# Low-rank mixing as four 32-row tiles in two visits per batch, and loads of q, k, v issued one per slot

## The chip, the cores and the metric

The kernel runs on one core of a Trainium2 chip. The core has TensorE (matmuls, PE in the profile, with its weight loads as PEld), VectorE (DVE), ScalarE (ACT), GpSimd (POOL) and SyncE (SP), which here only issues DMAs. The time is the device time of one execution in microseconds; of the kernel before it is 581.39 us, the median of five runs (579.47 to 582.15). A profiled execution is a run of its own.

## What is computed

The inputs are q, k and v of shape (8 batches, 12 heads, 448 positions, 64), two gains and the weights of a mixer. First comes attention with normalized q and k, then a mixer with a low-rank mixing over positions and a two-layer network over channels:

```python
q_n, k_n = rmsnorm(q, g_q), rmsnorm(k, g_k)
attn = softmax(q_n @ k_n.transpose / sqrt(64))
x = (attn @ v), heads side by side          # (8, 448, 768)
xt = x.transpose(0, 2, 1)
h = xt @ U @ V                              # U (448, 32), V (32, 448): the low-rank mixing
u = x + h.transpose(0, 2, 1)
ch = np.maximum(u @ w_ch1, 0.0) @ w_ch2     # 768 -> 3072 -> 768
out = u + ch
```

The change touches the two lines with h and u, and the loads of q, k and v.

## The kernel before

**Batches woven together.** While the channel network of batch b runs on TensorE ("fill", the generator `mlp`), the attention of batch b+1 and then its mixing are put between the pieces of that fill. The fill comes in chunks of six matmuls; a chunk of the first layer (ph) has 384 columns per matmul in even batches and 512 in odd ones, every other chunk (pa, pb, pe, po: the second layer) has 384. An even batch after the first has 24 + 22 = 46 chunks, 17664 columns in all, an odd one 24 chunks of 512 and 28 of 384, 23040 columns. `weave` places a list of weighted items into this fill: an item's due point is the running sum of weights times the columns allotted, whole chunks are emitted until that point is reached, then the item. The count starts anew for each list. `FA` gives the share of the columns allotted to the attention (its first number for an even fill, its second for an odd one, `FA0` for batch 0), `FM` that allotted to the mixing; the chunks left after that close the batch. The order of instructions on every engine is the order in which this code emits them.

**Attention.** A tile t is four heads, a slot p two heads. A slot consists of scores (L273, two heads as two 64-row tiles of TensorE), exponentials on ScalarE (L278), and the values of the slot before (L299) with a reciprocal and two multiplies on VectorE (L302 to L306). The normalization of later tiles runs beside: squares (L223, ScalarE), sums (L231, VectorE), scale (L244, VectorE, which makes qkn and frees the buffers of q and k). From slot 14 on (`NPE`) the transposes of qkn into qkT are DMA transposes on SP (L261); `gains` (L265, VectorE) then multiplies q's half, and the scores of that slot wait for it. q and k share three load buffers (tag "qk"), v has one (tag "vt").

**SP's queue.** The loads (L198, L209), the DMA transposes of qkT (L261) and of u (L346) and the stores of the output (L380) are all issued by SP in program order; one that waits holds up all behind it. In each odd slot SP gets three loads one after another: q of tile t+2, v of tile t+2, k of tile t+3.

**Mixing.** Each batch's 448 positions are held as four position tiles of 128 rows (`OFFS`; one of them is an edge, of which half the rows belong to the batch). For batches 1 to 7, `mix_t` multiplies each position tile with its part of U into 32 rows of a PSUM tile: position tile i goes to rows 32i to 32i+31, 128 x 32 tiles of TensorE, two halves of 384 channels. ScalarE copies the result to t4b (L325). So the four partial sums over positions lie one below the other, and V4 holds V four times: `mix_u` sums them by the contraction over 128 rows (L337), two matmuls of 384 columns per position tile, into a PSUM tile of the tag "s" (two buffers, shared with the scores). VectorE adds it to x in one operation (L339) and `mix_uT` issues a DMA transpose of that position tile into u (L346). In an even batch the fourth tile, the edge, isn't transposed; an odd batch transposes all four. u is read by the next batch's ph matmuls, all columns at once. Batch 0 has its own way (`mix_a`, `mix_b`), and the four calls of `mix_u` for batch 0 finish its x in the slots 7 to 10.

**Second layer.** `pair` computes two position tiles together with seven products instead of eight: VectorE forms differences and sums of activations between the products (A11 at L429, A12 at L440, act_sum1 and act_sum3 at L399 and L404), adds x to the outputs (o11 at L442, o12 at L455, o21 at L462) and SP stores them in up to three pieces each. PSUM for fill and products has three buffers (tag "mm"); the values use one buffer of the tag "o", except for the last slot's second head.

Of the kernel before, what the change touches and what calls it, by code (L numbers as in the profile page):

```python
# [9 lines left out]
FP32 = mybir.dt.float32  # L10
BF16 = mybir.dt.bfloat16
AX = mybir.AxisListType.X
AF = mybir.ActivationFunctionType
# [4 lines left out]
def kernel(  # L18
# [13 lines left out]
    nc = tc.nc  # L32
    B, H, S, D = q.shape
    dm = H * D
    dh = moe_w_ch1.shape[1]
    rank = moe_U.shape[1]
    assert (B, H, S, D) == (8, 12, 448, 64)

    P = 128
# [3 lines left out]
    KH = dh // P  # L43
    HG = 4
    HALF = dm // 2
    PAD = 64

    OFFS = ([0, 128, 256, 384], [-64, 64, 192, 320])  # L50
# [14 lines left out]
    upool = ctx.enter_context(tc.tile_pool(name="upool", bufs=1))  # L65
    opool = ctx.enter_context(tc.tile_pool(name="opool", bufs=5))
    ps_mm = ctx.enter_context(tc.tile_pool(name="ps_mm", bufs=3, space=bass.MemoryType.PSUM))
    ps_s = ctx.enter_context(tc.tile_pool(name="ps_s", bufs=2, space=bass.MemoryType.PSUM))
    ps_o = ctx.enter_context(tc.tile_pool(name="ps_o", bufs=1, space=bass.MemoryType.PSUM))
# [5 lines left out]
    NC = KH // 2  # L75
    Tw = consts.tile([P, 3, NC, HALF], BF16, name="Tw")
    S1 = consts.tile([P, NC, P], BF16, name="S1")
# [5 lines left out]
    Ub = consts.tile([P, 2, 4, rank], BF16, name="Ub")  # L83
    V4 = consts.tile([P, S], BF16, name="V4")
    Vsh = consts.tile([P, 2, P], BF16, name="Vsh")
# [2 lines left out]
    one = consts.tile([1, 1], FP32, name="one")  # L88
    eps = consts.tile([SP, 1], FP32, name="eps")
    NWARM, NH = 16, 2  # L90
    FA, FM, NPE, FA0 = (0.74, 0.77), 0.09, 14, 0.66
    flat = Tw.rearrange("p f c n -> p (f c n)")
    lent = [0]

    def lend(p, shape, dtype):

        n = 1
        for d in shape:
            n *= d
        n *= 2 if dtype == FP32 else 1  # L100
        a = flat[0:p, lent[0]:lent[0] + n]
        lent[0] += (n + 15) // 16 * 16
        a = a.bitcast(FP32) if dtype == FP32 else a
        names = "abcd"[:len(shape)]
        return a if len(shape) == 1 else a.rearrange(
            f"p ({' '.join(names)}) -> p {' '.join(names)}", **dict(zip(names, shape)))

    EW, VW = [2, PAD + NJ * S + PAD], [HG, NJ, D + 1]
    Es = [consts.tile([SP, *EW], BF16, name=f"E{i}") for i in range(2)] + [lend(SP, EW, BF16)]
# [10 lines left out]
    def setup():  # L120
# [5 lines left out]
        for t in Es:  # L126
            nc.gpsimd.memset(t[:, :, 0:PAD], 0.0)
            nc.gpsimd.memset(t[:, :, PAD + NJ * S:], 0.0)
        for t in xss:
# [14 lines left out]
    Uc = lend(SP, [NJ * rank], BF16)  # L144
    UT = lend(rank, [PAD + S + PAD], BF16)
    Vf = lend(P, [S], FP32)
# [12 lines left out]
    def setup_u(step):  # L159
        if step == 0:  # L160
            pt = ps_mm.tile([rank, S], BF16, tag="mm")
            for j in range(NJ):
                nc.tensor.transpose(pt[:, j * SP:(j + 1) * SP], Uc[:, j * rank:(j + 1) * rank], ident[:SP, :SP])
            nc.vector.tensor_copy(UT[:, PAD:PAD + S], pt)
        else:
            pt = ps_mm.tile([P, 2, 4, rank], BF16, tag="mm")
            for par in range(2):
                for i, off in enumerate(OFFS[par]):
                    nc.tensor.transpose(pt[:, par, i, :], UT[:, PAD + off:PAD + off + P], ident[:rank, :rank])
            nc.vector.tensor_copy(Ub, pt)  # L170
# [8 lines left out]
    def load_w2(half, i):  # L179
        c, d = slice(8 * i, 8 * (i + 1)), slice(half * HALF, (half + 1) * HALF)  # L180
        nc.gpsimd.dma_start(w2b[:, c, d], w2r[:, c, d])


    NT, NP = B * 3, B * 6
# [125 lines left out]
    t4s, us = {}, {}  # L310

    def x_tiles(b):
        xs = xss[(b // 2) % 2]
        full = [x3_of[b][:, i, :] for i in range(3)]
        return full + [xs] if b % 2 == 0 else [xs] + full

    def mix_t(b):
        xt = x_tiles(b)
        t4b = upool.tile([P, dm], BF16, tag="t4b", name="t4b")
        pm = ps_s.tile([P, 2, 512], FP32, tag="s", name="pm")  # L320
        for half in range(2):
            for i in range(4):
                nc.tensor.matmul(pm[i * rank:(i + 1) * rank, half, 0:HALF], Ub[:, b % 2, i, :],
                                 xt[i][:, half * HALF:(half + 1) * HALF], start=True, stop=True)
        nc.scalar.activation(t4b.rearrange("p (h n) -> p h n", h=2), pm[:, :, 0:HALF], AF.Copy)  # L325
        t4s[b] = t4b

    def mix_u(b, i, halves=(0, 1)):

        par, off = b % 2, OFFS[b % 2][i]  # L330
        lhsT = V4[:, off:off + P] if 0 <= off < 384 else Vsh[:, par, :]
        rows = slice(0, P) if 0 <= off < 384 else slice(64 * par, 64 * par + 64)
        xt = x_tiles(b)[i]
        n, hs = len(halves), slice(halves[0] * HALF, (halves[-1] + 1) * HALF)
        pu = ps_s.tile([P, 2, 512], FP32, tag="s", name="pu") if b else ps_mm.tile([P, n, HALF], FP32, tag="mm")
        for k, half in enumerate(halves):
            nc.tensor.matmul(pu[:, k, 0:HALF], lhsT, t4s[b][:, half * HALF:(half + 1) * HALF], start=True, stop=True)  # L337
        xv = xt[rows, hs].rearrange("p (h n) -> p h n", h=n)
        nc.vector.tensor_add(xv, pu[rows, 0:n, 0:HALF], xv)  # L339

    def mix_uT(b, i):
        par, off = b % 2, OFFS[b % 2][i]
        if i == 0:
            us[b] = upool.tile([P, KD, 384 + 128 * par], BF16, tag="u", name="u")
        if par or off < 384:
            nc.sync.dma_start_transpose(us[b][:, :, i * P:(i + 1) * P],  # L346
                                        x_tiles(b)[i].rearrange("t (c d) -> t c d", d=P))
# [168 lines left out]
    def attention(b, extra={}):  # L516

        items = []

        def add(weight, fn, *args):  # L520
            items.append((weight, lambda: fn(*args)))

        def idle():
            pass

        def sums(p, n):
            f = {12: 0, 13: 1, 14: 3, 15: 2}.get(p)
            if f is not None:
                add(0, weight_sums, f, 3 * n)

        for p in range(b * 6, b * 6 + 6):
            t, odd = divmod(p, 2)
            more, more2 = t + 1 < NT, t + 2 < NT
            add(2 if p == 6 else 1, scores, p, (0, 1))
            add(0, expo, p, 0)
            add(.5, expo, p, 1)
            if p + 1 < NP and (p + 1 >= NPE or not odd):
                add(.5, transposes, p + 1)
            if 7 <= p <= 10:
                add(0, mix_u, 0, p - 7, (0,))  # L540
            sums(p, 0)
            if not odd and more:
                add(0, squares, t + 1, ALL, (1,))
            if odd and more2:
                add(0, squares, t + 2, ALL, (0,))
            if p % 6:
                add(2, values, p - 1, 0)
            elif b > 1:
                add(1, idle)
            sums(p, 1)  # L550
            if not odd and more:
                add(0, reduce, t + 1, ALL, (1,))
            if odd and more:
                add(0, scale, t + 1, 1)
                add(0, yield_port, t + 1, 1)
                add(0, cast_v, t + 1)
            if odd and p > 6:
                if 6 <= t + 2 < NT:
                    add(0, load, t + 2, 1, (1,))
                    add(0, load_v, t + 2)  # L560
                if t + 3 < NT:
                    add(0, load, t + 3, 1, (0,))
            add(1, scores, p, (2, 3))
            add(0, expo, p, 2)
            add(.5, expo, p, 3)
            if p + 1 < NPE and odd:
                add(.5, transposes, p + 1)
            if 7 <= p <= 10:
                add(0, mix_u, 0, p - 7, (1,))
            if p + 1 < NP:  # L570
                add(0, gains, p + 1)
            if not odd and more:
                add(0, rsqrt, t + 1)
            sums(p, 2)
            if p % 6:
                add(1.5, values, p - 1, 1)
            elif b > 1:
                add(1, idle)
            sums(p, 3)
            if not odd and more:  # L580
                add(0, scale, t + 1, 0)
                add(0, yield_port, t + 1, 0)
            if odd and more2:
                add(0, reduce, t + 2, ALL, (0,))
            if p in extra:
                add(0, *extra[p])
        add(2, values, b * 6 + 5, 0)
        add(2, values, b * 6 + 5, 1)
        return items
# [145 lines left out]
            nc.scalar.activation(hT[:, 2 * i:2 * i + 2, 0:384], ph[:, :, 0:384], AF.Relu)  # L735

    def mixing(b):
        items = [(1, lambda: mix_t(b))]
        for i in range(4):
            items.append((1, lambda i=i: (mix_u(b, i), mix_uT(b, i))))  # L740
        return items

    def weave(fill, total, items):
# [62 lines left out]
```

## Time and profile before

| | |
|---|---|
| median of five runs | 581.39 us (579.47 to 582.15) |
| the profiled execution | 583.15 us, its span 581.4 us, mean granted clock 0.991 |
| TensorE busy | 563.1 us, 97% of the span |
| VectorE, ScalarE, GpSimd busy | 397.0, 280.6, 78.4 us |
| ph matmuls (L488) | 1107, 231.0 us |
| mixing: pu matmuls (L337) | 64, of 326 ns each; those of 384 columns for batches 1 to 7 are 56 of them |
| mixing: additions on VectorE (L339) | 28 of 768 columns, 0.95 us each, and 8 of 384, 0.55 us each |
| mixing: copy to t4b (L325) | 7 of 0.81 us |
| DMA transposes | 34 of qkT, 3.2 us median from issue to landing; 25 of u, 2.8 us |
| loads of q, k, v on SP | 448 KB each, 3.9 to 6.2 us median from issue to landing |

Busy time of TensorE counts a matmul from its start to its modelled end, and matmuls overlap in the pipeline; where TensorE follows at full rate, the distance of the starts is the cost. "Idle before" in a timeline's brackets is time in which the engine had nothing in flight, with what ended it. A wait in SP's own queue is no loss in itself, as SP mostly has nothing to do.

### The profile page before, as it was taken

How to read it: one execution, taken by the hardware profiler on the slowest of the kernel's cores; microseconds unless marked ns; L12 is line 12 of the kernel's file. 1: busy time of each engine (PE TensorE's matmuls, PEld its weight loads, DVE VectorE, ACT ScalarE, POOL GpSimd, SP SyncE). 2: the span in 40 equal slices, each digit the busy share in tenths (PEclk: the TensorE clock that was granted, in tenths of full speed). 3: DMA queues.
4: the chain of work that ended last, by engine and by line, in shares of the span. 5: the costliest groups of instructions: out<-in, count | busy, mean ns of one | idle time of the engine just before them, and what ended most of it. 6: DMA issues, size and time to landing. Idle time of an engine off the chain costs nothing.

```text
span 581.4 us, 11339 instructions
## 1 busy us (share of the span) xinstructions
PE 563.1 (97%) x4590; PEld 307.8 (53%) x4613; DVE 397.0 (68%) x811; ACT 280.6 (48%) x413; POOL 78.4 (13%) x122
## 2 busy tenths in 40 slices
PE   7899999999999999999999999999999999999997
PEld 2465556544465555544456555544456555554464
DVE  5867987389975687747777498756767587453342
ACT  5865673177621876166651677237661386302200
POOL 5651421000020001000020001000002010000010
PEclk9789999999999999999999999999999999999999
DMA  8999998515563355635536355556245431040021
GB/s 215 248 240 235 207 172 161 126 39 104 112 167 83 82 122 112 156 85 119 120 79 137 86 125 117 145 118 121 60 92 158 104 96 33 29 109 0 1 55 54
DMA packets 103648, 67.22 MB, mean 116 GB/s; under 512 B 54716, under 2 KB 102060, under 8 KB 103596
## 3 DMA queue, kind: packets, MB, share of 16 engines
q1 hardware_dynamic: 93988, 56.77, 41.8%
q0 software_dynamic: 9376, 9.44, 10.0%
q8 instruction: 36, 0.59, 0.4%
q10 hardware_dynamic: 232, 0.30, 0.2%
q14 instruction: 16, 0.13, 0.1%
HBM read 52.19 MB, written 11.01 MB: 109 GB/s over the span
## 4 chain that ended last, share of the span: by engine, by line
PE 84%; DVE 7%; DMA 4%; ACT 3%; issue 1%; POOL 1%; DVEq 0%; POOLq 0%; ACTq 0%
PE ph L488 34%; PE pb L413 10%; PE o L299 7%; PE pe L413 7%; PE po L413 7%; PE sc L273 7%; PE pa L413 6%; DMA qkT<-qkn 3%; ACT E L278 2%; PE pu L337 2%; DVE qkn L244 2%; PE warm L759 1%; PE pt L257 1%; PE first L732 1%; DMA u<-x 1%
## 5 line engine op out<-in xcount | busy, mean ns | idle before, releaser
L488 PE MATMUL ph<-u,w1b 128*128 128x384 bf16 (+1 forms) x1107 | 231.0, 353 | 1.5
L278 ACT ACTIVATE E<-sc 112x896 bf16<-112x896 f32 x184 | 160.1, 915 | 59.9 <-PE sc L273 58.3
L488 PEld LDWEIGHTS <-w1b 128*128 128x128 bf16 x1128 | 102.8, 98 | 108.6 <-issue 22.5
L413 PEld LDWEIGHTS <-hT 128*128 128x128 bf16 x1080 | 101.3, 98 | 71.5 <-issue 8.8
L491 ACT ACTIVATE hT<-ph 128x384 bf16<-128x384 f32 (+1 forms) x95 | 51.5, 543 | 136.2 <-PE ph L488 134.4
L493 DVE TENSOR_SCALAR hT<-ph 128x512 bf16<-128x512 f32 (+1 forms) x93 | 57.9, 622 | 53.2 <-PE ph L488 52.5
L299 PEld LDWEIGHTS <-E 112*128 112x128 bf16 x1472 | 59.8, 99 | 16.9 <-issue 1.9
L299 PE MATMUL o<-va,E 112*128 112x65 bf16 x1440 | 62.3, 196 | 0.8 <-DVE xs L306 0.8
L273 PE MATMUL sc<-qkT 64*128 64x448 bf16 x384 | 56.8, 362 | 4.8 <-ACT E L278 1.6
L244 DVE TENSOR_TENSOR qkn<-qk,rstd 112x512 bf16<-112x512 f32 x84 | 55.7, 701 | 8.0 <-ACT rstd L237 4.2
L720 POOL COPY scratch<-qkn 1x1 bf16<-1x1 bf16 x44 | 11.7, 265 | 311.0 <-DVE qkn L244 302.5
L413 PE MATMUL po<-w2b,hT 128*128 128x384 bf16 x288 | 52.5, 326 | 0.6 <-DVE hT L493 0.6
L231 DVE TENSOR_REDUCE rstd<-sq 112x16 f32<-112x1024 f32 x40 | 48.5, 1212 | 4.8 <-ACT sq L223 4.1
L413 PE MATMUL pa<-w2b,hT 128*128 128x384 bf16 x264 | 49.5, 326 | 0.0
L413 PE MATMUL pb<-Tw,hT 128*128 128x384 bf16 x264 | 48.0, 326 | 0.0
L223 ACT ACTIVATE sq<-qk 112x1024 f32<-112x1024 f32 x36 | 38.3, 1063 | 2.3 <-issue 1.1
L303 DVE TENSOR_TENSOR x<-o,rec 128x192 bf16<-128x192 f32 x96 | 34.3, 357 | 3.7
L448 POOL TENSOR_TENSOR o<-o,x 128x384 f32<-128x384 f32 x11 | 12.6, 1144 | 161.2 <-DVE o L447 161.2
L302 DVE RECIPROCAL rec<-o 128x4 f32<-128x4 f32 x96 | 17.0, 177 | 24.6 <-PE o L299 24.2
L273 PEld LDWEIGHTS <-qkT 64*128 64x128 bf16 x384 | 12.7, 94 | 36.8 <-issue 31.8
L428 ACT ACTIVATE pb<-pa 128x384 f32<-128x384 f32 x11 | 5.2, 475 | 50.4 <-PE pa L413 50.4
L339 DVE TENSOR_TENSOR x<-pu,x 128x768 bf16<-128x768 f32 (+1 forms) x27 | 23.3, 865 | 7.2 <-PE pu L337 7.0
(106 smaller groups left out, 450.7 us busy)
## 6 DMA issues: line engine op xcount, KB each, us to landing
qk<-in_k_dram SPq DMA_DIRECT2D x21, 448.0 KB, 6.2
vt<-in_v_dram SPq DMA_DIRECT2D x20, 448.0 KB, 5.1
qk<-in_q_dram SPq DMA_DIRECT2D x19, 448.0 KB, 3.9
w2b<-in_moe_w_ch_dram POOLq DMA_DIRECT2D x6, 768.0 KB, 9.4
w1b<-in_moe_w_ch_dram POOLq DMA_DIRECT2D x2, 1536.0 KB, 21.1
out_dram<-o SPq DMA_DIRECT2D x15, 168.0 KB, 2.7
out_dram<-o SPq DMA_DIRECT2D x16, 144.0 KB, 2.1
out_dram<-o SPq DMA_DIRECT2D x15, 120.0 KB, 2.5
```

Of the source, the lines that this page charges most:

```text
L223: nc.scalar.activation(sqs[t, s][:, hs], qks[t, s][:, hs], AF.Square)
L231: nc.vector.tensor_reduce(rstds[t][:, s, hs].rearrange("p h j -> p (h j)"), sqs[t, s][:, hs].rearrange("p h (j d) -> p (h j) d", d=D), AX, ...
L244: nc.vector.tensor_tensor(qkn[:, s].rearrange("p j h d -> p h j d"), qks[t, s][:, hp].rearrange("p h (j d) -> p h j d", d=D), rstd[:, s, h ...
L273: nc.tensor.matmul(sc[:, hh, 0:S], kT[pp, kc * SP:kc * SP + P], qT[pp, :], start=True, stop=True)
L278: nc.scalar.activation(E_of(p)[:, :, PAD + kc * S:PAD + (kc + 1) * S], scs.pop((p, kc))[0:SP, :, 0:S], AF.Exp, scale=float(D) ** 0.5)
L299: nc.tensor.matmul(o[:, i, :], E[:, hh, c:c + P], va[:, hl, kc, :], start=(kc == 0), stop=(kc == NJ - 1))
L303: nc.vector.tensor_tensor(x3[:, :, d0:d0 + D], o[:, t0:t0 + 3, 0:D], rec[:, t0:t0 + 3].rearrange("p c -> p c ()").to_broadcast([P, 3, D]), ...
L339: nc.vector.tensor_add(xv, pu[rows, 0:n, 0:HALF], xv)
L413: nc.tensor.matmul(ps, lhs[:, c, :], rhs[:, c, :], start=first and c == 0, stop=last and c == NC - 1, skip_group_check=again)
L488: nc.tensor.matmul(ph, w1b[:, dc, hc * P:(hc + 1) * P], u[:, dc, :], start=(dc == 0), stop=(dc == KD - 1))
L491: nc.scalar.activation(hT[:, hc, 0:n], ph, AF.Relu)
L493: nc.vector.tensor_relu(hT[:, hc, 0:n], ph)
```

## The change

Three things are changed together.

- `mix_t` sums over the position tiles in PSUM instead of laying them below each other. Now rows 32j to 32j+31 hold channel block j (192 channels), and the four position tiles accumulate there: 16 matmuls of 192 columns instead of 8 of 384. The result t4b has 192 columns instead of 768. It lies in the buffer of the tag "o".
- `mix_us` takes two position tiles per visit. For each it runs four matmuls with 32 rows of contraction, one per channel block j, on the four row tiles of TensorE, each into a PSUM bank of its own (two PSUM tiles of the tag "s" with two banks each). VectorE then adds them to x in two operations of 384 columns per position tile, and the DMA transposes follow per position tile. The items' weights are 0.4, 1.2 and 2.0 instead of five ones, FA falls by 0.02 and FM rises by 0.02.
- The loads of a tile go out one at a time: k of tile t+2 in the even slot, behind that slot's transposes; q of tile t+2 in the odd slot where the three were; v of tile t+2 at the end of the odd slot.

```diff
--- before.py
+++ after.py
@@ -43,6 +43,7 @@
     KH = dh // P
     HG = 4
     HALF = dm // 2
+    BLK = dm // 4
     PAD = 64
 
 
@@ -88,7 +89,7 @@
     one = consts.tile([1, 1], FP32, name="one")
     eps = consts.tile([SP, 1], FP32, name="eps")
     NWARM, NH = 16, 2
-    FA, FM, NPE, FA0 = (0.74, 0.77), 0.09, 14, 0.66
+    FA, FM, NPE, FA0 = (0.72, 0.75), 0.11, 14, 0.66
     flat = Tw.rearrange("p f c n -> p (f c n)")
     lent = [0]
 
@@ -316,14 +317,33 @@
 
     def mix_t(b):
         xt = x_tiles(b)
-        t4b = upool.tile([P, dm], BF16, tag="t4b", name="t4b")
-        pm = ps_s.tile([P, 2, 512], FP32, tag="s", name="pm")
-        for half in range(2):
-            for i in range(4):
-                nc.tensor.matmul(pm[i * rank:(i + 1) * rank, half, 0:HALF], Ub[:, b % 2, i, :],
-                                 xt[i][:, half * HALF:(half + 1) * HALF], start=True, stop=True)
-        nc.scalar.activation(t4b.rearrange("p (h n) -> p h n", h=2), pm[:, :, 0:HALF], AF.Copy)
+        t4b = upool.tile([P, BLK], BF16, tag="t4b", name="t4b", padded_shape=[P, dm])
+        pm = ps_o.tile([P, BLK], FP32, tag="o", name="pm", padded_shape=[P, 4 * (D + 1)])
+        for i in range(4):
+            for j in range(4):
+                nc.tensor.matmul(pm[j * rank:(j + 1) * rank, :], Ub[:, b % 2, i, :],
+                                 xt[i][:, j * BLK:(j + 1) * BLK], start=(i == 0), stop=(i == 3))
+        nc.scalar.activation(t4b, pm, AF.Copy)
         t4s[b] = t4b
+
+    def mix_us(b, i0):
+
+        par = b % 2
+        pus = [ps_s.tile([P, 2, 512], FP32, tag="s", name="pu") for _ in range(2)]
+        for k in range(2):
+            off = OFFS[par][i0 + k]
+            edge = not 0 <= off < 384
+            for j in range(4):
+                r = slice(j * rank, (j + 1) * rank)
+                nc.tensor.matmul(pus[j // 2][:, j % 2, k * BLK:(k + 1) * BLK],
+                                 Vsh[r, par, :] if edge else V4[r, off:off + P], t4s[b][r, :], start=True, stop=True)
+        for k in range(2):
+            off = OFFS[par][i0 + k]
+            rows = slice(0, P) if 0 <= off < 384 else slice(64 * par, 64 * par + 64)
+            for h in range(2):
+                xv = x_tiles(b)[i0 + k][rows, h * HALF:(h + 1) * HALF].rearrange("p (j n) -> p j n", j=2)
+                nc.vector.tensor_add(xv, pus[h][rows, :, k * BLK:(k + 1) * BLK], xv)
+            mix_uT(b, i0 + k)
 
     def mix_u(b, i, halves=(0, 1)):
 
@@ -539,6 +559,8 @@
             if 7 <= p <= 10:
                 add(0, mix_u, 0, p - 7, (0,))
             sums(p, 0)
+            if not odd and p > 7 and t + 2 < NT:
+                add(0, load, t + 2, 1, (0,))
             if not odd and more:
                 add(0, squares, t + 1, ALL, (1,))
             if odd and more2:
@@ -554,12 +576,8 @@
                 add(0, scale, t + 1, 1)
                 add(0, yield_port, t + 1, 1)
                 add(0, cast_v, t + 1)
-            if odd and p > 6:
-                if 6 <= t + 2 < NT:
-                    add(0, load, t + 2, 1, (1,))
-                    add(0, load_v, t + 2)
-                if t + 3 < NT:
-                    add(0, load, t + 3, 1, (0,))
+            if odd and p > 6 and 6 <= t + 2 < NT:
+                add(0, load, t + 2, 1, (1,))
             add(1, scores, p, (2, 3))
             add(0, expo, p, 2)
             add(.5, expo, p, 3)
@@ -582,6 +600,8 @@
                 add(0, yield_port, t + 1, 0)
             if odd and more2:
                 add(0, reduce, t + 2, ALL, (0,))
+            if odd and p > 6 and 6 <= t + 2 < NT:
+                add(0, load_v, t + 2)
             if p in extra:
                 add(0, *extra[p])
         add(2, values, b * 6 + 5, 0)
@@ -735,9 +755,9 @@
             nc.scalar.activation(hT[:, 2 * i:2 * i + 2, 0:384], ph[:, :, 0:384], AF.Relu)
 
     def mixing(b):
-        items = [(1, lambda: mix_t(b))]
-        for i in range(4):
-            items.append((1, lambda i=i: (mix_u(b, i), mix_uT(b, i))))
+        items = [(.4, lambda: mix_t(b))]
+        for i in (0, 2):
+            items.append((1.2 + .4 * i, lambda i=i: mix_us(b, i)))
         return items
 
     def weave(fill, total, items):
```

## Prediction

> **What bounds the kernel now.** I read the page first (busy shares, the chain that ended last), then the busy time by stretch, then the timeline of one mixing and of the slots before it.
>
> ```profile
> span 581.4 us, 11339 instructions
> ...
> PE 563.1 (97%) x4590; PEld 307.8 (53%) x4613; DVE 397.0 (68%) x811; ACT 280.6 (48%) x413; POOL 78.4 (13%) x122
> ...
> PE 84%; DVE 7%; DMA 4%; ACT 3%; issue 1%; POOL 1%; DVEq 0%; POOLq 0%; ACTq 0%
> ```
>
> TensorE is busy 97% of the span and 84% of the chain. So only two things can move the time: columns that TensorE no longer streams, and gaps between its matmuls. The stretches tell where the gaps are.
>
> ```profile
> 188.00:250.00 62.00, 60.03 (x529) 34.05 (x528) 45.62 (x93) 34.33 (x51) 5.57 (x10) 1.00 0.55 119
> 290.00:325.00 35.00, 35.00 (x287) 20.50 (x286) 24.29 (x49) 9.68 (x16) 4.40 (x5) 1.00 0.47 109
> 325.00:385.00 60.00, 59.13 (x523) 33.78 (x523) 45.53 (x93) 33.85 (x51) 5.57 (x10) 1.00 0.54 123
> ```
>
> The columns are length, then PE, PEld, DVE, ACT and POOL busy. The two stretches in which batches 2 and 4 fill TensorE leave 1.97 and 0.87 us idle, the one from an odd batch's fill 0.00. The granted clock is 1.00 in all three. Now the cause in the first one, from its timeline:
>
> ```profile
> 214.88 0.31 SPq L198 DMA_DIRECT2D qk<-in_q_dram  x1
> ...
> 216.73 0.31 SPq L209 DMA_DIRECT2D vt<-in_v_dram  x1
> ...
> 217.15 0.43 SPq L198 DMA_DIRECT2D qk<-in_k_dram  x1
> ...
> 217.67 1.22 SPq L261 DMA_TRANSPOSE qkT<-qkn  x1
> ...
> 224.80 0.34 DVE L265 TENSOR_SCALAR qkT<-qkT,gg 128x448 bf16<-128x448 bf16 x1 [1.36 <-DMA qkT<-qkn]
> ...
> 225.28 0.55 PE L273 MATMUL sc<-qkT 64*128 64x448 bf16 x4 [0.63 <-DVE qkT L265]
> ```
>
> Three loads of 448 KB go out on SP within 3 us, and the transpose queued behind them lands late. VectorE stands in front of the gain multiply (1.36 us), TensorE behind it (0.63). The chain gives the transposes' flight: 7.11 us here, 2.97 us for one with no load in front.
>
> ```profile
> 217.67 7.11 DMA qkT<-qkn
> ...
> 229.70 2.97 DMA qkT<-qkn
> ```
>
> And the mixing itself, with the boundary to the next batch:
>
> ```profile
> 238.33 0.34 PE L323 MATMUL pm<-x,Ub 128*32 128x384 bf16 x3
> ...
> 238.51 0.33 PE L323 MATMUL pm<-x,Ub 128*32 128x384 bf16 x3
> ...
> 238.77 1.15 PE L413 MATMUL pb<-Tw,hT 128*128 128x384 bf16 x6
> ...
> 239.76 0.49 PE L337 MATMUL pu<-t4b,Vsh 128*128 128x384 bf16 x2
> ...
> 240.08 1.14 PE L413 MATMUL pb<-Tw,hT 128*128 128x384 bf16 x6
> ...
> 243.66 0.49 PE L337 MATMUL pu<-t4b,V 128*128 128x384 bf16 x2
> ...
> 243.86 0.96 DVE L440 TENSOR_TENSOR hT<-hT 128x1536 bf16<-128x1536 bf16 x1
> ...
> 244.73 0.55 DVE L442 TENSOR_TENSOR o<-pa,x 128x384 f32<-128x384 f32 x1
> ...
> 245.20 0.95 DVE L339 TENSOR_TENSOR x<-pu,x 128x768 bf16<-128x768 f32 x1
> ...
> 246.64 1.21 SPq L346 DMA_TRANSPOSE u<-x  x1
> ...
> 249.83 1.46 PE L488 MATMUL ph<-u,w1b 128*128 128x512 bf16 x5
> ```
>
> To be seen: a position's two matmuls (pu) cost TensorE 0.32 us (239.76 to 240.08). The last position is computed at 243.66, its transpose goes out at 246.64, and the next batch's first matmul, which needs all of u, starts at 249.83.
>
> **The change part by part.**
>
> (1) *Mixing on TensorE.* Full rate is 1.95 us for 12 matmuls of 384 columns (chain, "pe L413 x12"), 162 ns each, so 81 ns for 192 columns. The four pm matmuls of a half start within 0.01 us and the next four 0.17 us later: column tiles run together. After them the old code has 8 pu matmuls per batch, 4 x 0.325 = 1.30 us, full width, without a change of tiling. A change of tiling costs: the six pe matmuls from 237.26 should end at 238.24, pm starts 0.09 later; pm takes 0.44 to the next product where two waves need 0.325; together 0.2 us a block. New: per visit two waves of four matmuls with 32 rows, 2 x 81 ns + 0.2 + some 0.03 of issue = 0.39 us, against 0.65 for two old positions. This supposes that four row tiles run together; the scores (two 64-row tiles) do, as their block of four takes 0.49 us (251.22 to 251.71) where four serial passes would need 0.76. Saved 0.26 x 14 visits (batches 1 to 7) = 3.6 us. The projection (mix_t) becomes four waves of 81 ns in place of two of 162; its weight loads (94 ns each) could hold a wave a little, so I add 0.05 x 7. Term: -3.3 us. Bounds: -4.1 (no issue cost, no weight hold) and +3.1 (row tiles run one by one: 8 x 81 ns + 0.2 = 0.85 a visit). I take the value near the scores, the nearest row.
>
> The Trainium skill, "TensorEngine Tiling (Array Packing)", section Tiling Modes, says that changing the tiling mode drains TensorE (key properties), which speaks against this change, as each visit now switches there and back. The trace agrees with 0.2 us around pm. The page's theoretical speedup (section Overview) of up to 4 for 32 rows would make the 1.30 us into 0.33 and the term -6.8; the drains measured in this trace cut it to about half.
>
> (2) *Loads between the transposes.* The k load for tile t+3 leaves the group of three and is issued after the next slot's transpose; v stays behind q, as in most slots SP has nothing else between. The next transpose thus queues behind two loads instead of three; a third of 7.11 - 2.97 = 4.1 us is 1.4, and by the landings in the median (k 6.2 us, v 5.1, issued 0.4 apart) 1.5. The multiplies that now wait 1.1 to 1.9 us (the view of waits: 6.6 us in 5 waits of DVE on qkT) come through nearly on time. No buffer wait is added: k's buffer was freed a slot before, so SP is blocked for less. What is late next: ScalarE's squares of k, now about one slot (some 7 us at 217) after the load's issue instead of two; the load needs 4 to 6. At a batch's first slot the load goes out at about 190.0 (transpose at 188.76 plus 1.27), the squares come at 196.16: enough for 4, just not for 6.2, and then ScalarE (55% busy there) absorbs most. Of the 2.84 us idle in the two stretches, 0.24 at 202.04 and its twin in batch 4 are VectorE's own backlog and stay: 2.84 - 0.48. Term: -2.3 us, bounds 0 and -2.8. The waits at 233.94 (0.52) and 235.77 (0.17) count in it: there the transpose stands behind an output store and now moves ahead of it by a chunk.
>
> (3) *Two positions per visit at the batch boundary.* Even fill, counted in chunks of 384 columns: 46 in all. Old: attention takes 0.74 x 17664 columns, 35 chunks; the last position follows chunk 40. New: 34 chunks, mixing due after 216, 864 and 1943 columns more, chunks 35, 37 and 40. So the last visit stays where it was, six chunks (5.85 us) before the next batch, but it holds two positions with four additions. From s = 243.66: A12 s+0.2, o11 s+1.07, additions of 128x384 (0.55 us, one each 0.47) at s+1.54, 2.01, 2.48, 2.95. SP issues o11's two stores from s+1.9 to 2.9, then the transpose of position 2 (1.21 us; formerly before the stores) at 3.0 and that of position 3 at 4.3; landing 2.8 us after (median of the DMA issues) is s+7.1. TensorE is there at s+6.2. So 0.85 us of stall at each of three boundaries (into batches 3, 5, 7): +2.5 us. Bounds 0 (DMA quicker) and +5 (flight 3.6). Odd fill: visit after chunk 44 of 52 instead of 45, eight left, and the even batch's u needs only position 2: nothing. Batch 0's fill: likewise, nothing.
>
> (4) *The projection's inputs.* Attention ends a chunk or two earlier. In even fills the last values now fall just behind VectorE's A11 (0.96 us); their four small operations (0.6 us) end some 0.2 us after TensorE could start mix_t. In odd fills o12 and act_sum3 (0.55 + 0.94) come before them: about 0.1. Term: +0.7 with rounding (3 x 0.2 + 3 x 0.05), bounds 0 and +2.
>
> (5) *Others.* t4b's eviction shrinks on ScalarE from 0.81 us to below the 0.48 of a copy of 384 columns: hidden, as the additions follow two chunks later. VectorE does 8 additions of 0.55 for 4 of 0.95 per batch, +0.6 us; behind TensorE except in (3). pm in the o buffer: its last reader feeds the same x, no new wait. Denser attention: +0.1, bounds 0 and +1.5.
>
> Sum: -3.3 - 2.3 + 2.5 + 0.7 + 0.1 = -2.3 us. The profiled execution took 583.15 us, 1.77 around its span, and stands 1.8 above the median 581.39. So 580.85 for it, **579.1** as a median. 0.3% (1.7 us) is about what the runs here can tell from no change: five of them spread over 2.7 us.
>
> **The rivals.**
>
> A. *u late eats the gain.* At the last boundary of the trace the chain has 3.44 us of flight for u's last transpose (from 515.51), and TensorE already waits some 0.3 us at 518.99. With that flight everywhere, 1.5 us a boundary instead of 0.85, +2.0: 581.1, no change. For it: stores share the queue there. Against it: at 246.64 the flight fits into the 3.19 us up to 249.83.
>
> B. *The loads change nothing.* VectorE's waits are replaced by others (a backlog as at 202.04, ScalarE waiting for k): the 2.3 are lost, 581.4. For it: VectorE is 74% busy in that stretch. Against it: in the stretches of odd batches, where the transposes are in time, TensorE doesn't wait.
>
> C. *Slower: four row tiles do not run together.* Only two 64-row tiles are seen to. Serial, term 1 is +3.1 instead of -3.3: 585.5. It decides from a visit of about 0.67 us on (579.1 + 14 x 0.28 = 583.0); with pairs in step, 0.52 a visit, the time is 580.9.
>
> D. *All good.* Boundaries in time, everything else as above: 576.6.
>
> **How the numbers follow.** Forecast and D: 0.52 (0.40 and 0.12), all faster. A and B with C's half case: 0.25, the same. C in full, or A at flight times over 4 us at all boundaries together with the upper end of (4) (about 584): 0.23, slower. The range leaves out the most extreme of D and part of C: 575.5 to 584.5; the forecast's own is 577.5 to 580.7.
>
> **What would show it.** Right: pu matmuls of 32x128 starting within 0.02 us four by four and a visit of 0.35 to 0.45 us; transposes of qkT in no case over 5.5 us in flight; the wait at 225 gone; before the first ph of batches 3, 5, 7 a wait for DMA u of 0.5 to 1.2 us. Wrong: pu starts 80 ns apart (C); ScalarE waiting for qk loads; DVE waiting for qkT as before (B); boundary waits above 1.5 us (A) or none (D). What would make the forecast wrong most easily is that terms 1 and 3 nearly cancel and both rest on timings not in the trace.

## The result and the profile after

The changed kernel takes 582.93 us (median of 44 runs, 580.19 to 589.03), the kernel before 581.37 us (79 runs): a ratio of 1.0027, with a 95% interval of 1.0019 to 1.0036. It is 1.6 us slower, 1.1 to 2.1. The forecast was 2.3 us faster. The time lies in the forecast's range, but it moved the other way.

The profiled executions seem to say the opposite: the span is 580.1 us after and 581.4 before. The stretch of the head, which the change doesn't touch, explains it. Busy time by stretch, the kernel before:

```profile
13.00:49.00 36.00, 31.37 (x366) 18.57 (x367) 27.59 (x72) 23.19 (x31) 19.22 (x20) 0.86 1.14 241
```

and the kernel after (the third number from the end is the granted clock):

```profile
13.00:49.00 36.00, 30.78 (x382) 18.31 (x385) 29.51 (x76) 24.85 (x36) 19.10 (x21) 1.00 1.14 240
```

In the execution before, TensorE had 0.86 of its clock in this stretch, and its first chunk of the first layer (ph) starts at 48.86 us instead of 46.62. From there to the last matmul it is 528.7 us before and 529.7 after: 1.0 us slower, the same way as the timed runs. All that follows compares parts from such a landmark to the next, or ratios of timed runs.

The busy shares of the page, the changed kernel:

```profile
span 580.1 us, 11590 instructions
...
PE 557.9 (96%) x4702; PEld 303.5 (52%) x4725; DVE 394.5 (68%) x839; ACT 276.6 (48%) x413; POOL 75.3 (13%) x122
...
PE 82%; DVE 11%; ACT 3%; DMA 2%; issue 2%; POOL 1%; DVEq 0%; POOLq 0%; ACTq 0%
```

TensorE is busy 5.2 us less than before, 0.6 of it in the head, but is not done sooner: VectorE's share of the chain went from 7 to 11%. Busy time by stretch shows where TensorE stands now (length, then PE busy):

```profile
188.00:250.00 62.00, 60.26 (x545) 33.70 (x546) 45.52 (x98) 33.52 (x52) 4.97 (x10) 1.00 0.56 125
290.00:325.00 35.00, 34.84 (x292) 19.87 (x291) 22.22 (x47) 10.34 (x16) 3.80 (x5) 1.00 0.48 109
325.00:385.00 60.00, 58.12 (x532) 32.76 (x532) 44.26 (x97) 31.39 (x49) 4.97 (x10) 1.00 0.49 121
```

Idle are 1.74, 0.16 and 1.88 us (before 1.97, 0.00 and 0.87). The gaps have new places. The timeline of the mixing in the fill of batch 2:

```profile
232.41 0.36 DVE L304 TENSOR_TENSOR x<-o,rec 128x192 bf16<-128x192 f32 x1
...
232.59 0.26 PE L324 MATMUL pm<-xs,Ub 128*32 128x192 bf16 x3
...
232.78 0.23 DVE L307 TENSOR_TENSOR xs<-o,rec 64x64 bf16<-64x64 f32 x1
...
233.06 0.24 PE L324 MATMUL pm<-xs,Ub 128*32 128x192 bf16 x1 [0.21 <-DVE xs L307]
...
233.48 1.15 PE L433 MATMUL pe<-Tw,S 128*128 128x384 bf16 x6
...
238.84 0.34 PE L338 MATMUL pu<-t4b,V 32*128 32x192 bf16 x8
238.95 0.96 DVE L460 TENSOR_TENSOR hT<-hT 128x1536 bf16<-128x1536 bf16 x1 [0.47 <-PE pa L433]
...
239.83 0.55 DVE L462 TENSOR_TENSOR o<-pa,x 128x384 f32<-128x384 f32 x1
240.29 1.94 DVE L345 TENSOR_TENSOR x<-pu,x 128x384 bf16<-128x384 f32 x4
240.40 1.59 SPq L400 DMA_DIRECT2D out_dram<-o  x2
...
242.09 2.54 SPq L366 DMA_TRANSPOSE u<-x  x2
...
246.28 1.46 PE L508 MATMUL ph<-u,w1b 128*128 128x512 bf16 x5 [1.14 <-DMA u<-x]
```

Three things are to be seen. The projection starts at 232.59, gets three matmuls out, and stands until VectorE has written the last x (232.78 + 0.23), so that its fourth starts at 233.06. The second visit's eight matmuls at 238.84 are short: the next product starts 0.28 us later. And behind that visit stand, in this order, A12, o11, the four additions, o11's two stores and two transposes; TensorE is through its work at 244.98 (the last twelve matmuls start at 243.03 and take 1.95) and starts the next batch at 246.28. In the list of waits this is a new line (by the starts, the kernel before loses 0.3 us at the last boundary and nothing at the others):

```profile
PE ph L508 <- DMA u<-x: 4.1, 3, 1.7
```

VectorE's wait for qkT behind a DMA (6.6 us before) has gone from that list. The chain gives the flight of the transpose that ends each of the three boundaries, 2.8 us twice and 4.2 at the last:

```profile
243.39 2.76 DMA u<-x
...
378.83 2.79 DMA u<-x
513.53 4.18 DMA u<-x
```

### The profile page after: what moved, and what is told of

Its sections match the earlier page's. It is cut to its first block, busy times and chain, and to the rows that moved or that the text cites. A ratio compares the mean times of both kernels' runs of the same rounds, so it can differ in the third digit from the quotient of the medians.

```text
span 580.1 us, 11590 instructions
## 1 busy us (share of the span) xinstructions
PE 557.9 (96%) x4702; PEld 303.5 (52%) x4725; DVE 394.5 (68%) x839; ACT 276.6 (48%) x413; POOL 75.3 (13%) x122
## 4 chain that ended last, share of the span: by engine, by line
PE 82%; DVE 11%; ACT 3%; DMA 2%; issue 2%; POOL 1%; DVEq 0%; POOLq 0%; ACTq 0%
PE ph L508 34%; PE po L433 8%; PE pb L433 8%; PE pa L433 8%; PE sc L274 7%; PE o L300 7%; PE pe L433 6%; DVE qkn L245 2%; ACT E L279 2%; DMA u<-x 2%; DVE rstd L232 1%; DVE x L304 1%; DVE hT L424 1%; PE warm L779 1%; DVE hT L460 1%
## 5 line engine op out<-in xcount | busy, mean ns | idle before, releaser
L300 PEld LDWEIGHTS <-E 112*128 112x128 bf16 x1472 | 58.4, 98 | 15.5 <-DVE xs L307 1.3
L245 DVE TENSOR_TENSOR qkn<-qk,rstd 112x512 bf16<-112x512 f32 x84 | 57.7, 724 | 6.8 <-issue 3.3
L300 PE MATMUL o<-va,E 112*128 112x65 bf16 x1440 | 61.0, 194 | 0.0
L740 POOL COPY scratch<-qkn 1x1 bf16<-1x1 bf16 x44 | 8.9, 202 | 307.5 <-DVE qkn L245 303.9
L433 PE MATMUL pa<-w2b,hT 128*128 128x384 bf16 x264 | 47.1, 327 | 0.0
L433 PE MATMUL pe<-Tw,S 128*128 128x384 bf16 x132 | 24.3, 327 | 0.0
L433 PE MATMUL pb<-w2b,hT 128*128 128x384 bf16 x132 | 23.8, 327 | 0.0
```

Source lines behind the costliest of these rows:

```text
L245: nc.vector.tensor_tensor(qkn[:, s].rearrange("p j h d -> p h j d"), qks[t, s][:, hp].rearrange("p h (j d) -> p h j d", d=D), rstd[:, s, h ...
L300: nc.tensor.matmul(o[:, i, :], E[:, hh, c:c + P], va[:, hl, kc, :], start=(kc == 0), stop=(kc == NJ - 1))
L433: nc.tensor.matmul(ps, lhs[:, c, :], rhs[:, c, :], start=first and c == 0, stop=last and c == NC - 1, skip_group_check=again)
```

## The experiments

Read from the two traces by the distances of TensorE's starts, the change is a sum of four terms: tiles -3.5 us, gaps around qkT and the values -2.1, waits for u +4.3, waits in the projection +2.2. These are first readings; the runs below put the tiles at -3.8 and the projection at +2.5. The experiments undo or repair one of them each. Ratios are to the kernel before, timed beside it; 0.1% is 0.58 us.

### The loads alone

```diff
-            if odd and p > 6:
-                if 6 <= t + 2 < NT:
-                    add(0, load, t + 2, 1, (1,))
-                    add(0, load_v, t + 2)
-                if t + 3 < NT:
-                    add(0, load, t + 3, 1, (0,))
+            if not odd and p > 7 and t + 2 < NT:
+                add(0, load, t + 2, 1, (0,))
...
+            if odd and p > 6 and 6 <= t + 2 < NT:
+                add(0, load, t + 2, 1, (1,))
...
+            if odd and p > 6 and 6 <= t + 2 < NT:
+                add(0, load_v, t + 2)
```

> The kernel before with nothing but the moved loads (k in the even slot, q and v in the odd one); mixing, FA and FM are the old ones. Theory T (the change is a sum of four terms, read from the two profiles: tiles -3.5 us, loads -2.1, waits for u at three boundaries +4.3, waits in the projection's matmuls +2.2): 2.1 us faster than before, 579.3, and VectorE's waits for qkT (6.6 us in the kernel before) under 2 us. Rival L (the loads give nothing; the gaps of batch 2 in the profile before belong to that one execution or come back elsewhere): 581.4, no change.

Measured: 0.9992 (0.9974 to 1.0009), 0.5 us faster and not told from nothing. The waits of VectorE in this run:

```profile
DVE qkT L265 <- DMA qkT<-qkn: 3.9, 3, 1.8
```

Of 6.6 us in five waits 3.9 us in three are left, where under 2 was expected. The gap before the scores at 225 us is gone, those in front of the values in the fills of batches 2 and 4 (0.39 and 0.34 us at 232 and 234, 0.42 and 0.34 at 367 and 369) stayed. So the rival is nearer: with the old attention the loads are worth little, and those other gaps are not theirs.

### The mixing with the old loads

```diff
-            if not odd and p > 7 and t + 2 < NT:
-                add(0, load, t + 2, 1, (0,))
...
+            if odd and p > 6:
+                if 6 <= t + 2 < NT:
+                    add(0, load, t + 2, 1, (1,))
+                    add(0, load_v, t + 2)
+                if t + 3 < NT:
+                    add(0, load, t + 3, 1, (0,))
```

> The changed kernel with the loads put back where they were, three together in the odd slot. Theory T: the loads' 2.1 us are lost, 585.0 against 582.9 of the changed kernel, 0.6% slower than before. Rival L: 582.9, as the changed kernel.

Measured: 1.0113 (1.0089 to 1.0138), 6.6 us slower than before and 5.0 slower than the changed kernel. Both theories missed: the loads are worth 0.5 us in the old kernel and 5.0 in the new one. The timeline shows what they prevent there:

```profile
212.20 0.31 SPq L199 DMA_DIRECT2D qk<-in_q_dram  x1
...
214.05 0.31 SPq L210 DMA_DIRECT2D vt<-in_v_dram  x1
...
214.47 0.43 SPq L199 DMA_DIRECT2D qk<-in_k_dram  x1
...
214.99 11.52 SPq L262 DMA_TRANSPOSE qkT<-qkn  x2
...
222.84 0.34 DVE L266 TENSOR_SCALAR qkT<-qkT,gg 128x448 bf16<-128x448 bf16 x1 [2.60 <-DMA qkT<-qkn]
...
223.32 0.55 PE L274 MATMUL sc<-qkT 64*128 64x448 bf16 x4 [2.33 <-DVE rec L303]
```

The flights in its chain:

```profile
214.99 7.83 DMA qkT<-qkn
...
353.41 8.02 DMA qkT<-qkn
```

It is the picture of the kernel before, with TensorE standing 2.33 us instead of 0.63; at 361.94 it is 1.89 again. Not all of the 5.0 us is waiting: in this trace the granted clock falls just after the first of these gaps, to 0.67 from 224 to 226 us and 0.50 from 226 to 228, which lost some 1.7 us by an estimate from these two rows. No such drop follows the gap at 361.94. In all six timed runs of this kernel the mean clock lies between 0.994 and 0.997, while 18 of the 29 runs of the kernel before beside it have 0.999 or more, so such a drop probably belongs to most of them; what sets it off was not tested. The scores come earlier, the transpose doesn't. New in this kernel are the mixing and the denser attention (FA); the next two runs tell which.

### The denser attention alone, and with the loads

```diff
-    FA, FM, NPE, FA0 = (0.74, 0.77), 0.09, 14, 0.66
+    FA, FM, NPE, FA0 = (0.72, 0.75), 0.11, 14, 0.66
```

In the kernel before, first with its old loads:

> The kernel before with FA 0.72 and 0.75 and FM 0.11, and nothing else: old mixing, old loads. Tells what the denser attention does by itself with three loads in front of a transpose. Theory D (the waits for qkT at 223 and 362 us in the run with the mixing only, 2.5 and 2.1 us, come from the denser attention): the same two waits here, and the gaps before the values in batches 2 and 4 (0.65 + 0.34 and 0.41 + 0.34 us) gone: +4.5 - 0.9 - 1.7 = +1.9, 583. Rival: the waits belong to the new mixing; 579.5 to 581, no wait for qkT above 1 us.

Measured: 1.0015 (0.9989 to 1.0041). The time is not told from either, the list of waits is:

```profile
DVE qkT L265 <- DMA qkT<-qkn: 4.8, 5, 1.4
...
PEld L273 <- DMA qkT<-qkn: 3.8, 3, 1.6
```

TensorE now waits for the transposes itself (3.8 us; before 1.6), in the old mixing too: 1.28 us at 225, 1.40 at 361, some 0.57 each at 345 and 353. The gaps in front of the values are gone, as expected. From the first ph to the last matmul this trace takes 530.6 us, 1.9 more than before, but one execution each doesn't settle it. Then with the moved loads:

> The kernel before with the moved loads and the new FA and FM, and the old mixing: everything of the change but the mixing. Theory D (the denser attention is what the loads' move pays for): the waits for qkT of the run with FA alone (1.28, 1.40, 0.56 and 0.58 us lost at TensorE) are gone and the gaps before the values stay gone, 3.8 us faster than that run, ratio to the kernel before about 0.995, 578.5. What is then left of the change, the mixing in two visits, costs -3.5 + 4.3 - 0.5 + 2.2 = +2.5 us on top. Rival: the loads are worth 0.6 us here as in the run with the loads only, ratio 1.000.

Measured: 0.9977 (0.9955 to 0.9999), 1.3 us faster than before, about half of what was expected; in its list of waits there is none for a transpose of qkT. From one batch's first chunk to the next, its trace takes 60.58 us for each of the fills of batches 2 and 4 (before 62.73 and 61.50). From the first ph to the last matmul it takes 526.4 us, 2.3 less than before; the trace of before may hold more of these gaps than its usual run, which no run here settles. In this trace the moved loads and the denser attention belong together: the denser attention removes the gaps in front of the values, the moved loads keep qkT in time for it. Everything but the mixing is a gain of 1.3 us (0.1 to 2.6), and the mixing costs the difference to 1.0027: 2.9 us, where -3.5 + 4.3 - 0.5 + 2.2 = 2.5 was expected.

### The last visit one chunk earlier

```diff
-    FA, FM, NPE, FA0 = (0.72, 0.75), 0.11, 14, 0.66
+    FA, FM, NPE, FA0 = (0.72, 0.75), 0.108, 14, 0.66
```

> The changed kernel with FM 0.108 instead of 0.11. By the due points this moves one thing: in the three even fills the second visit comes after chunk 39 instead of 40, so ahead of A12, of o11 and of o11's stores; every other item stays. Theory T: the wait for u before the first ph of batches 3, 5 and 7 (1.14 us idle in the first, 4.3 us of lost starts in all) is gone, and a wait of up to 0.3 us per even batch for the score buffers at the second visit may come: 4.3 - 0.6 = 3.7 us faster than the changed kernel, 579.2. Rival Q (the flight of the transposes and SP's queue set the boundary, not the order behind A12 and the stores): the wait for u stays above 0.7 us each, 581 or more.

Measured: 0.9968 (0.9947 to 0.9988), 3.4 us faster than the changed kernel. Its timeline in the same place:

```profile
237.88 0.53 PE L338 MATMUL pu<-t4b,V 32*128 32x192 bf16 x8
...
238.30 4.57 SPq L366 DMA_TRANSPOSE u<-x  x3
...
238.40 1.94 DVE L345 TENSOR_TENSOR x<-pu,x 128x384 bf16<-128x384 f32 x4
...
240.26 0.94 DVE L460 TENSOR_TENSOR hT<-hT 128x1536 bf16<-128x1536 bf16 x1
...
242.97 3.80 SPq L400 DMA_DIRECT2D out_dram<-o  x8
...
245.18 1.46 PE L508 MATMUL ph<-u,w1b 128*128 128x512 bf16 x5
```

The additions now stand in front of A12 and the transposes in front of o11's stores; the first ph starts without a wait, 1.1 us sooner. The visit takes 0.46 us instead of 0.28, the announced wait for the score buffers. Theory T holds, with 3.4 for 3.7.

### o11's store from ScalarE's queue

```diff
-        store(b, i, 0, o11)
+        store(b, i, 0, o11, (nc.scalar,) if b % 2 == 0 else (nc.sync,))
```

> The changed kernel with the store of o11 (first output of the pair) issued by ScalarE instead of SP in even batches. Splits the wait for u into its two causes: SP's queue (o11's stores in front of the two transposes) and VectorE (A12 and o11 in front of the additions). By the timeline of the changed kernel the second position's transpose would go out at about 241.4 instead of 242.1 (its additions end at 241.3) and the third's 1.3 later: the wait at the three boundaries falls by some 0.7 us each, from 4.3 to 2.2 us in sum, 580.9. If SP's queue is all of it: 579. If VectorE is all of it: 582.9, no change.

Measured: 0.9995 (0.9979 to 1.0011), 1.9 us faster than the changed kernel, where 2.1 was expected. By the starts of its matmuls, the three boundaries lose 0.39, 0.67 and 1.57 us instead of 1.30, 1.43 and 1.89 (its profiled execution had a granted clock of 0.949, so these are rough). So about half of the wait came from SP's queue and the rest from what stands before on VectorE, and at the last boundary from a flight that is 1.3 us longer than the others (4.07 against 2.78).

### The projection one chunk later

```diff
-        items = [(.4, lambda: mix_t(b))]
+        items = [(.8, lambda: mix_t(b))]
         for i in (0, 2):
-            items.append((1.2 + .4 * i, lambda i=i: mix_us(b, i)))
+            items.append((.8 + .6 * i, lambda i=i: mix_us(b, i)))
```

> The changed kernel with the mixing's weights 0.8, 0.8, 2.0 instead of 0.4, 1.2, 2.0. By the due points the projection alone moves, one chunk later in every batch; the two visits stay. Theory T: the gap inside the projection's matmuls (0.33 to 0.39 us in six batches, 2.2 us in all, TensorE waiting for VectorE's last x) is gone: 2.2 us faster than the changed kernel, 580.7. Rival M (the gap is a price of the sixteen column-tiled matmuls or moves to the visit, which now follows one chunk after the projection's copy): 582.4 to 582.9, a gap of 0.3 us in the projection or before the first visit.

Measured: 0.9975 (0.9958 to 0.9992), 3.0 us faster than the changed kernel, where 2.2 was expected. Timeline:

```profile
232.60 0.23 DVE L307 TENSOR_TENSOR xs<-o,rec 64x64 bf16<-64x64 f32 x1
...
233.38 0.27 PE L324 MATMUL pm<-xs,Ub 128*32 128x192 bf16 x4
233.47 0.42 PE L324 MATMUL pm<-x,Ub 128*32 128x192 bf16 x12
...
233.83 1.15 PE L433 MATMUL pb<-Tw,hT 128*128 128x384 bf16 x6
```

The last x is written 0.55 us before the projection starts, the sixteen matmuls run through in 0.45 us, and no gap comes at the visit. The gap was a wait for VectorE, not a price of the tiles. Against these 0.45 us the sixteen matmuls of the changed kernel take 0.84 to 0.90 us up to the next product in six batches. That is 2.5 us lost, more than the 2.2 read off first.

### Both moves

> The changed kernel with FM 0.108 and weights 0.8, 0.8, 2.0: the last visit of even fills one chunk earlier and the projection one chunk later in all. Theory T: the two gains add, ratio to the kernel before 1.0027 - 0.0059 - 0.0052 = 0.992, some 576.5 us against 581.1; no wait for u, no gap in the projection. Rival K (with both, the visits and the projection crowd VectorE or the score buffers, and part comes back): 0.995 or above.

Measured: 0.9919 (0.9898 to 0.9940), a median of 577.18 us. The two gains add. Busy time by stretch:

```profile
188.00:250.00 62.00, 60.94 (x551) 34.14 (x551) 45.89 (x99) 34.36 (x53) 4.98 (x10) 1.00 0.62 127
290.00:325.00 35.00, 35.00 (x294) 20.07 (x293) 22.63 (x48) 10.73 (x17) 3.80 (x5) 1.00 0.47 111
325.00:385.00 60.00, 59.43 (x538) 33.19 (x538) 44.82 (x99) 32.72 (x50) 4.98 (x10) 1.00 0.55 123
```

This is the fastest version found, faster than both kernels. It also gives the tiles' worth by itself in the odd fills, where nothing waits in either: from first chunk to first chunk they take 73.07 us here and 73.61 with the old mixing (the run with loads and FA), 0.54 us a batch. In time it is 0.58%, 3.4 us (some 1.7 either way), ahead of that run. In the even fills something still waits. The second visit takes 0.46 us, as in the run that has it earlier, and in the fill of batch 2 one transpose of qkT flies 7.30 us behind two loads and TensorE stands for it:

```profile
214.42 7.30 DMA qkT<-qkn
...
222.22 0.56 PE L274 MATMUL sc<-qkT 64*128 64x448 bf16 x4 [0.65 <-DVE rec L303]
```

So the moved loads do not keep every transpose in time.

### One position per visit

```diff
-        for k in range(2):
+        for k in range(1):
...
-        items = [(.4, lambda: mix_t(b))]
-        for i in (0, 2):
-            items.append((1.2 + .4 * i, lambda i=i: mix_us(b, i)))
+        items = [(1, lambda: mix_t(b))]
+        for i in range(4):
+            items.append((1, lambda i=i: mix_us(b, i)))
```

> The changed kernel with one position per visit (four visits of four 32-row matmuls, weights all 1, as the old mixing was placed). By the due points even fills then have the projection after chunk 36 and positions after 37, 38, 39, 40. Each visit is one wave of 81 ns and the change of tiling there and back (0.2): 0.29 us instead of 0.37 for two, so +0.42 us a batch, +2.9 us; the wait for u falls as in the kernel before (-4.0) and the gap in the projection goes (-2.2): 579.6. If the change of tiling costs nothing, the visits are 0.1 us and the time 576.7 or less; if it costs more than 0.2, 581 or more.

Measured: 1.0040 (1.0019 to 1.0061), 583.7 by the ratio, 4 us above the expectation. The price of the tilings was right: a visit whose four matmuls are not held up takes 0.19 us to the next product and 0.10 before it, 0.29 as expected. Something else was missed:

```profile
240.80 1.15 PE L433 MATMUL pa<-w2b,hT 128*128 128x384 bf16 x6
241.88 0.26 PE L338 MATMUL pu<-t4b,V 32*128 32x192 bf16 x2
242.34 0.26 PE L338 MATMUL pu<-t4b,V 32*128 32x192 bf16 x2 [0.21 <-DVE x L345]
242.53 1.15 PE L433 MATMUL pa<-w2b,hT 128*128 128x384 bf16 x6
```

Four row tiles write into four banks, that is both score buffers, for one position as for two. The next visit, one chunk later, gets the second buffer only when VectorE's second addition has read it, and its wave breaks in two: 0.65 us to the next product (241.88 to 242.53) instead of 0.19. In odd fills the first half waits too (0.41 us before it instead of 0.10). By the starts these are some 5 us in the seven batches, and the boundaries into batches 5 and 7 still lose 0.22 and 0.97: more than the 4 us that are missing, in the trace of one execution. The Trainium skill's page "TensorEngine Tiling (Array Packing)", under PSUM Bottleneck, says that tiling speeds up the matmuls but not the emptying of PSUM; the break at 242.34 is a case of it.

## Why the prediction was wrong, by its steps

The steps that failed are (3) and (4): together put at +3.2 us, they measured +6.8. Their mechanism was right and their size was not. Term (2) credited the loads with gaps that are not theirs. Slower had been given 0.23, for row tiles that run one by one or for flights over 4 us at all boundaries with the upper end of (4). Of these only the last came, 2.5 us against +2.

**(1) Mixing on TensorE, -3.3: right.** Four row tiles do start together, a visit costs 0.28 us and 0.10 before it (0.39 forecast). The projection without its gap, in the run that has it later, costs 0.54 us (231.34 + 1.95 to 233.83) where the old one had 0.53. That makes 2 x (0.65 - 0.37) - 0.01 = 0.55 a batch, and the distances of the odd fills under "Both moves" say 0.54: 3.8 us in seven batches, a little more than forecast. The change of tiling, there and back, costs the 0.2 us of the row before. Rival C is refuted.

**(2) Loads, -2.3: this term was put together wrongly.** Most flights shortened (the longest in the changed kernel is 5.93 us, above the 5.5 named as a sign), and no load came late for ScalarE. But the 2.3 us were the idle time of two stretches in one profiled execution, and the waits at 233.94 and 235.77 went into the loads' account, though the loads alone leave them (run with the loads only). They go with the denser attention, and the denser attention with the old loads gains nothing (1.0015). Loads and attention together gave 1.3 us in time (0.1 to 2.6), 2.3 by the distance from the first ph to the last matmul in two traces.

**(3) Two positions per visit, +2.5: right mechanism, mis-sized.** The order on VectorE and SP was as written down. Measured were 1.30, 1.43 and 1.89 us, 4.6 in sum and 4.3 more than before, for 0.85 each. At each boundary one DMA step ran longer than in the sum, and not the same one. At the first, o11's two stores held SP for 1.59 us instead of 1.00. So the transpose of the second position went out 3.25 us after the second visit's start (3.0 forecast) and the next 1.3 later; TensorE was through after 6.14 instead of 6.2. At the other two:

```profile
375.66 0.79 SPq L400 DMA_DIRECT2D out_dram<-o  x2
376.59 3.48 SPq L366 DMA_TRANSPOSE u<-x  x2
...
511.29 0.79 SPq L400 DMA_DIRECT2D out_dram<-o  x2
512.22 2.54 SPq L366 DMA_TRANSPOSE u<-x  x2
```

Here the stores take 0.79 us. But at the second boundary the two transposes hold SP 3.48 instead of 2.54, and at the last the flight is 4.18 instead of 2.8. With 0.79, 2.54 and 2.8 everywhere each boundary would lose some 0.5 us, an estimate from these rows; the rest is the long steps: 0.8, 0.9 and 1.4. They are not chance of one execution: in the trace with the mixing only the stores at the first boundary take 1.45, the transposes at the second 3.79 and the last flight 4.22. Why these steps are long stays open. Rival A had asked for the 3.44 us flight of the kernel before at all boundaries; it came at the last alone, and longer.

**(4) The projection's inputs, +0.7: right mechanism, mis-sized by more than three.** Measured 0.39 us in each of three odd fills and 0.44 in each of three even ones, 2.5 us. VectorE's small operations (a reciprocal and two multiplies, three and not four) were counted from the end of A11 without the distances between them: they take 0.82 us from the first start (232.19) to the last end (233.01), not 0.6. The odd fills, put at 0.05 each, wait nearly as long. And the wait comes inside the projection: three matmuls out, then a gap.

**(5) Others, +0.1:** with the denser attention each of the three odd fills takes 0.1 us longer (73.61 against 73.52), so about +0.3, which is inside the 1.3 of (2).

With the measured sizes the sum is -3.8 - 1.3 + 4.3 + 2.5 = +1.7 us; timed were +1.6 (1.1 to 2.1). With 2.3 for (2), as in the traces, it is +0.7, where the traces differ by 1.0. The sign turned on (3) and (4), which I sized by short timings of single steps (1.00 us for two stores, 2.8 for a flight, 0.6 for three operations), while both are chains on VectorE and SP that TensorE waits for.

## What to carry to other kernels

Where TensorE is the bound, shortening its own work also shortens the cover of everything that runs beside it: here 3.8 us less of matmuls came with 6.8 us of new waits. Two positions of a due-time plan, one chunk each, turned a loss of 0.3% into a gain of 0.8%; so look at the order in which the other engines get their work behind a merged step before judging the merge. And parts of a change can be worth nothing or 5 us depending on the other part (the loads), so undo each in the company in which it runs.

## What the runs showed of the hardware

- A DMA transpose of qkT in SP's queue mostly flies 2.9 us (the median of those with no load in front, in either kernel), 3.7 to 7.3 with two loads of 448 KB issued in the 3.5 us before it, and 5.2 to 8.0 with three. The Trainium skill's page "DMA: Bandwidth & Descriptors" (Queues, rings and completion order) says that each DMA engine takes the descriptors of a ring in order; these flights fit that.
- The last transpose of u takes 3.4 to 4.5 us at the last boundary in the seven traces whose chain shows it, in a stretch in which no loads of q, k, v are left. At the first two boundaries of the changed kernel it takes 2.8, but 4.41 at the second with both moves and 3.74 with one position per visit. What it shares its time with there was not found.
- In six of the eleven traces TensorE has half its clock for 3 to 10 us near the start (0.86 on average over 36 us in the profile of before). The first ph then starts at 47.9 to 48.9 us; in the four traces with a full clock there it starts at 46.5 to 46.7. That is up to 2.2 us, more than the change itself, and must be taken out before two spans are compared. In the run with the mixing only the clock also fell to half behind a wait of 2.33 us.
